# A new order of all 4,839 instructions for a layer of attention and gated feed-forward

## The chip, the cores and the metric

The kernel runs on one core of one Trainium2 chip. The metric is the device time of one execution in microseconds (us), median of several runs. The core has a matrix engine (PE, with its weight loads shown as PEld), a vector engine (DVE), a scalar engine (ACT), GpSimd (POOL), and SyncE (SP), which here only issues DMAs. In this program each works off its own list of instructions in order; one that waits for a semaphore stands in front of all that follow it there.

## The reference

For x of 2048 rows and 512 columns (the factors and biases of the norms are none):

```python
h  = x + A(layernorm(x))                    # attention, 32 heads of 16, 4 segments of 512 rows
h2 = h + (gelu(n @ w_gate) * (n @ w_up)) @ w_down      # n = layernorm(h), inner width 1376
# A, for each segment s and head:
logits = qs @ ks.T * 16**-0.5 + mask        # causal inside the segment
o = g * (phi(qs) @ M) / (phi(qs) @ z + 1e-6) + (1 - g) * softmax(logits) @ vs
M, z = M + phi(ks).T @ vs, z + sum(phi(ks)) # memory of the segments before
# phi(t) = t+1 if t > 0 else exp(t);  g = sigmoid(beta);  at the end o @ wo
```

## The kernel before

All products that need it are made of operands split into a high and a low part ("slot" tiles hold both), three matmuls for one product. The attention is worked off in 16 units U (four columns of heads by four segments), each of two halves Q = 2U, 2U+1:

- `qkv(U)` projects q and k (matmuls of L938), evicts them, and moves them by DMA into the tiles stq and stk (L1062, L1068, L1075); `vproj` makes v (L987, for the first unit L1000).
- `pass_a(Q)` makes the logits once only for the row maxima: matmuls (L1192) into two PSUM banks, and for each block of a bank one DVE reduction (L1202). POOL splits the maxima (L1216, L1217), PE turns them (L1223), and a small DMA writes them into stq (L1230).
- `pass_b(Q)` makes the logits again, transposed (L1250), ACT takes the exponential (L1256), POOL sets the masked triangle to zero (L1264), and PE multiplies by v (L1278, "accum"). Later come the division and the sum with the memory's part (L1311 on DVE, L1317 on POOL).
- `mem(U)` reads the memory (L1140 to L1165).
- `split_weight` and `split_wv` load a weight and split it; for the later weights POOL makes both the high part (L668, L689) and the low part (L675, L694).

Then `wo_seg` makes the output projection, `ln2` the second norm with sums of blocks (L795, L1392, L1398, L1403), and `ffn`/`down` the feed-forward part with a Strassen-like scheme: `prod` (L1537) makes products of three matmuls, ACT copies them (L1544), DVE adds them (L1549), `geglu` (L1555 to L1569) the activation, and `down` (L1602) the last product, which DVE adds to the rows held (L1610). It runs in two halves of 1024 rows, p = 0 and 1.

What is computed, on which engine and from what is fixed by calls of a planner's `op`, which numbers them 0 to 4838 in the order in which the program text makes them (1247 of PE, 1189 of DVE, 1026 of ACT, 751 of POOL, 626 of SP's DMAs; a PE operation is a group of 2 to 32 matmuls). A list of numbers written out in the file, ORDER, then says in which order they are issued. All tiles but constants come from pools, among them the eight PSUM banks; an operation takes its buffers at its place in the order, from those that its predecessors have given back:

```python
        for i in order:
            o = self.ops[i]
            ...
            for v in o.vals:
                if v.t is None and v.pool is not None:
                    p = v.pool
                    v.t = p.free.pop(0)[2]
            ...
            o.fn()                                   # issues the instructions
```

`pass_a` takes two banks for a group of matmuls, and they come back when its DVE reductions are done:

```python
            sas = Val(PA), Val(PA)
            ...
            pe(sum(rr((i + 1) * P) for _, i, _ in cols), prio, f, [sq, sk], sas, acq=[nm], head=0.12, mode="r")
            for a, sa in enumerate(sas):
                for p, i, c0 in cols: ...            # one dve reduction (L1202) per block of the bank
```

The operations that the text names by number:

| number | engine | what |
|---|---|---|
| 5, 6 | SP | loads of the first two blocks of 128 rows of x |
| 2, 3 | POOL, DVE | two iotas (L612, L616); the mask made of them (L622 to L624) |
| 39, 41, 43 | DVE | low parts of the first norm's second half (L907) |
| 93 | POOL | low part of the first wk (L675), read by 102, the first projection (L959) |
| 113 | PE | part of the first projection, reads 39 |
| 123, 122, 124 / 140 | SP | moves of the first q / of the first k |
| 170 | PE | first group of `pass_a(0)` |
| 1461, 1463 | POOL | masks of `pass_b(13)` (L1264), read by 1479, an accum (L1278) |
| 2123, 2124 | POOL | high and low part of a later wv (L689, L694) |
| 2549 | DVE | reciprocal of the denominators of Q = 25 (L1311) |
| 2729, 2735, 2745 | PE | three groups of `pass_a(29)` (L1192) |
| 2736, 2737, 2738, 2739 | DVE | reductions of group 2735 (L1202), two on each of its banks |
| 2609, 2711 | PE | accums of Q = 26 and 27 (L1278) |
| 3066 to 3069 | DVE | normalized rows of `ln2`, one segment (L795) |
| 3838, 3839 | PE, DVE | a `down` product of the first half (L1602) and its addition (L1610) |
| 3842, 3845 | DVE | two more such additions |
| 4051, 4064 / 4055 / 4123 | DVE | block sums of `ln2` (L1392) / a low part (L1403) / a low part of the activation (L1569) |
| 4187 | PE | a `prod` of the second half's first tile (L1537), takes a new bank |
| 4100, 4101, 4105 | PE, ACT, PE | a `prod`, the copy of its bank (L1544), the `prod` that writes the bank again |

Of the kernel before, what the change touches and what calls it, by code (L numbers as in the profile page):

```python
# [56 lines left out]
    0, 6, 5, 100, 1, 10, 9, 8, 12, 7, 28, 13, 14, 91, 16, 4, 76, 11, 92, 27, 18, 29, 30, 15, 17, 31, 88, 89, 32,  # L57
    33, 93, 94, 34, 19, 44, 35, 164, 21, 95, 821, 23, 90, 97, 25, 20, 22, 47, 36, 24, 37, 102, 822, 38, 825, 84,
    77, 46, 103, 104, 82, 26, 110, 42, 826, 96, 43, 105, 39, 81, 111, 167, 40, 827, 106, 112, 823, 98, 107, 113,
    41, 99, 828, 108, 114, 51, 109, 78, 115, 116, 829, 87, 50, 117, 830, 128, 129, 45, 118, 119, 120, 831, 133,  # L60
    48, 121, 144, 631, 145, 123, 134, 122, 146, 49, 147, 832, 80, 135, 833, 139, 138, 52, 124, 834, 165, 53,
    166, 140, 168, 2, 169, 54, 130, 824, 3, 55, 75, 136, 835, 131, 137, 151, 132, 170, 181, 172, 150, 185, 57,
    127, 253, 186, 254, 255, 148, 256, 125, 59, 171, 190, 182, 189, 126, 176, 149, 1024, 184, 85, 58, 188, 1025,
    1027, 56, 152, 836, 187, 153, 257, 101, 74, 161, 163, 154, 837, 183, 180, 60, 1028, 177, 179, 61, 258, 178,
    173, 79, 83, 175, 634, 143, 67, 142, 838, 68, 174, 191, 192, 1029, 141, 62, 818, 259, 69, 260, 2986, 65,
    193, 66, 63, 64, 72, 73, 70, 195, 71, 261, 213, 215, 214, 194, 196, 217, 438, 839, 632, 633, 262, 263, 197,
    198, 199, 270, 216, 439, 440, 625, 272, 229, 840, 441, 239, 273, 1030, 264, 442, 269, 230, 266, 231, 232,
    242, 274, 271, 267, 265, 243, 233, 276, 203, 204, 205, 206, 207, 275, 240, 443, 86, 241, 224, 277, 841, 162,
    444, 227, 225, 268, 226, 234, 628, 842, 237, 278, 445, 200, 201, 245, 202, 238, 228, 843, 235, 248, 236,
    446, 280, 208, 209, 246, 210, 448, 211, 247, 449, 212, 155, 249, 1026, 279, 450, 156, 1031, 218, 447, 244,  # L70
    219, 250, 1032, 844, 220, 292, 221, 845, 222, 846, 157, 1033, 406, 251, 847, 848, 281, 1034, 849, 295, 286,
    294, 293, 288, 852, 287, 282, 635, 636, 1035, 407, 223, 297, 301, 283, 408, 300, 296, 298, 318, 319, 409,
    289, 299, 321, 328, 410, 329, 302, 331, 291, 411, 290, 304, 313, 303, 361, 362, 365, 412, 363, 626, 305,
    627, 314, 306, 307, 308, 316, 323, 413, 364, 320, 324, 353, 355, 354, 326, 414, 815, 1411, 315, 366, 367,
    368, 325, 369, 158, 252, 370, 1036, 797, 1037, 309, 330, 427, 798, 311, 317, 334, 799, 415, 327, 332, 416,
    159, 310, 312, 160, 356, 359, 357, 360, 322, 337, 429, 417, 335, 800, 358, 336, 430, 418, 629, 338, 630,
    421, 333, 1417, 420, 422, 428, 433, 432, 801, 434, 284, 339, 340, 419, 387, 388, 390, 437, 435, 341, 285,
    431, 350, 351, 352, 802, 371, 372, 392, 393, 389, 391, 377, 378, 380, 803, 398, 804, 373, 401, 374, 805,
    482, 375, 483, 484, 485, 486, 586, 376, 395, 396, 806, 426, 379, 394, 809, 587, 808, 477, 1038, 479, 381,
    478, 480, 481, 399, 436, 382, 807, 385, 386, 588, 514, 383, 466, 603, 467, 468, 589, 590, 342, 425, 384,  # L80
    402, 503, 515, 517, 850, 1039, 506, 469, 504, 470, 471, 344, 397, 345, 493, 472, 423, 474, 476, 475, 424,
    473, 507, 505, 400, 343, 494, 516, 496, 495, 591, 498, 592, 508, 346, 347, 497, 487, 501, 488, 541, 502,
    499, 593, 518, 2119, 509, 489, 543, 511, 491, 544, 594, 542, 510, 500, 512, 536, 540, 537, 1040, 348, 490,
    816, 1608, 817, 608, 595, 1041, 539, 545, 403, 492, 609, 597, 598, 538, 596, 610, 513, 614, 457, 615, 458,
    600, 613, 519, 520, 1224, 601, 404, 602, 405, 459, 611, 2113, 533, 599, 1225, 534, 535, 616, 578, 579, 1226,
    605, 781, 567, 581, 570, 571, 530, 1227, 617, 546, 612, 568, 531, 1228, 532, 607, 1042, 606, 549, 550, 572,
    548, 575, 576, 1229, 569, 573, 574, 562, 521, 547, 551, 563, 552, 564, 565, 566, 649, 651, 650, 1230, 557,
    767, 558, 559, 662, 663, 664, 560, 665, 561, 666, 853, 768, 580, 553, 555, 554, 556, 1231, 851, 646, 647,
    648, 1043, 1232, 604, 1233, 652, 653, 654, 655, 656, 785, 1234, 1235, 1236, 769, 657, 659, 660, 1044, 1045,
    658, 770, 673, 674, 771, 676, 661, 577, 582, 618, 460, 583, 688, 683, 584, 522, 523, 1046, 772, 689, 585,  # L90
    1047, 678, 349, 773, 1048, 1049, 1050, 1051, 691, 1052, 727, 819, 675, 820, 729, 667, 692, 677, 728, 731,
    686, 684, 668, 1414, 681, 774, 730, 685, 687, 669, 775, 679, 717, 670, 680, 694, 718, 1420, 719, 671, 690,
    720, 682, 721, 672, 776, 777, 778, 779, 780, 697, 695, 696, 788, 461, 462, 524, 786, 787, 791, 698, 789,
    693, 637, 792, 793, 525, 794, 526, 699, 463, 700, 638, 790, 464, 451, 465, 722, 1605, 1054, 784, 726, 701,
    725, 796, 724, 989, 452, 723, 714, 1609, 453, 1610, 1003, 1055, 795, 715, 738, 1056, 990, 716, 711, 739,
    783, 741, 991, 753, 713, 756, 992, 743, 712, 993, 754, 742, 746, 619, 621, 620, 782, 871, 872, 873, 994,
    759, 995, 879, 880, 881, 882, 883, 755, 747, 732, 740, 744, 527, 702, 748, 996, 762, 733, 760, 874, 875,
    876, 877, 878, 751, 1418, 749, 1419, 734, 997, 736, 854, 761, 745, 735, 884, 885, 886, 887, 888, 1008, 757,
    703, 752, 855, 750, 1010, 737, 1009, 998, 1011, 1014, 758, 2122, 639, 622, 704, 763, 1421, 623, 1422, 705,
    764, 765, 999, 1012, 1191, 856, 868, 869, 870, 857, 859, 860, 2989, 1192, 895, 896, 1013, 858, 528, 898,  # L100
    897, 529, 1193, 900, 901, 1194, 902, 910, 949, 903, 1195, 913, 914, 889, 1001, 890, 766, 953, 911, 905, 906,
    951, 950, 908, 1196, 944, 1197, 952, 706, 891, 916, 945, 1198, 893, 1018, 948, 947, 1015, 946, 917, 936,
    937, 1002, 907, 938, 1199, 861, 909, 919, 892, 899, 862, 904, 624, 1004, 912, 939, 1213, 918, 1214, 943,
    1000, 810, 863, 707, 942, 1200, 1201, 894, 811, 812, 866, 940, 920, 1215, 2995, 915, 941, 867, 864, 1415,
# [1600 lines left out]
```

## Time and profile before

| what | value |
|---|---|
| median of 3 runs | 746.55 us (746.38 to 747.04) |
| the profiled execution's own time | 746.22 us |
| its span, first to last instruction | 744.5 us |
| PE busy | 728.4 us, 98% |
| DVE, ACT, POOL busy | 568.1, 502.7, 485.5 us |

The busy times are sums over all instructions of an engine; the span is what the time follows. An engine's idle time is printed in brackets behind the instruction that ended it, with the instruction on another engine that released it. The busy time of PE counts a matmul to its modelled end, so gaps shorter than a matmul's tail do not show as idle.

### The profile page before, as it was taken

How to read it: one execution, taken by the hardware profiler on the slowest of the kernel's cores; microseconds unless marked ns; L12 is line 12 of the kernel's file. 1: busy time of each engine (PE TensorE's matmuls, PEld its weight loads, DVE VectorE, ACT ScalarE, POOL GpSimd, SP SyncE). 2: the span in 40 equal slices, each digit the busy share in tenths (PEclk: the TensorE clock that was granted, in tenths of full speed). 3: DMA queues.
4: the chain of work that ended last, by engine and by line, in shares of the span. 5: the costliest groups of instructions: out<-in, count | busy, mean ns of one | idle time of the engine just before them, and what ended most of it. 6: DMA issues, size and time to landing. Idle time of an engine off the chain costs nothing.

```text
span 744.5 us, 18739 instructions
## 1 busy us (share of the span) xinstructions
PE 728.4 (98%) x6496; PEld 583.4 (78%) x6496; DVE 568.1 (76%) x1812; ACT 502.7 (68%) x1058; POOL 485.5 (65%) x770
## 2 busy tenths in 40 slices
PE   7999999999999999999999999999999999999997
PEld 6888877877878777876768788888887878888886
DVE  7997889998886898899986656865777666565385
ACT  6888888797767868878685567665685454554540
POOL 6554446565627556897784788759798279659730
PEclk9999999999999999999999999999999999999999
DMA  7755667747666766766768656245353430000003
GB/s 254 216 144 134 175 183 184 192 124 200 165 172 173 210 189 174 216 199 175 206 198 271 231 186 167 56 104 135 120 149 115 145 120 2 0 1 1 0 1 114
DMA packets 89659, 107.93 MB, mean 145 GB/s; under 512 B 31468, under 2 KB 41884, under 8 KB 89564
## 3 DMA queue, kind: packets, MB, share of 16 engines
q1 hardware_dynamic: 89260, 106.34, 50.1%
q8 instruction: 51, 0.84, 0.5%
q10 hardware_dynamic: 304, 0.39, 0.2%
q14 instruction: 44, 0.36, 0.2%
HBM read 57.03 MB, written 23.53 MB: 108 GB/s over the span
## 4 chain that ended last, share of the span: by engine, by line
PE 49%; DVE 2%; ACT 1%; DMA 1%; issue 0%; DVEq 0%; SPq 0%; ACTq 0%
PE bank L1537 27%; PE bank L1602 15%; PE bank L1351 3%; PE bank L1358 2%; PE bank L1278 2%; PE bank L1250 1%; DVE row L1610 1%; DMA stq<-slot 1%; PE bank L1192 0%; DVE row L1564 0%; DVE bank L1392 0%; DVE bank L1562 0%; DVE bank L1549 0%; DVE row L1392 0%; DVE row L1557 0%
## 5 line engine op out<-in xcount | busy, mean ns | idle before, releaser
L1256 ACT ACTIVATE row<-bank 128x512 f32<-128x512 f32 x306 | 163.3, 607 | 34.8 <-PE bank L1250 25.7
L1264 POOL TENSOR_SCALAR_AFFINE_SELECT row<-row 128x256 f32<-128x256 f32 (+1 forms) x306 | 103.9, 363 | 87.7 <-ACT row L1256 82.6
L1202 DVE CUSTOM_DVE_ANT_0 aside<-bank,amask 128x128 f32<-128x128 f32 (+2 forms) x384 | 140.7, 419 | 17.7 <-PE bank L1192 11.7
L938 PE MATMUL bank<-slot,slot 64*128 64x512 f32 x720 | 115.3, 403 | 0.5 <-DVE z L1151 0.2
L1537 PE MATMUL bank<-slot,slot 128*128 128x512 f32 (+1 forms) x357 | 95.2, 390 | 0.7 <-DVE row L1610 0.7
L1202 DVE CUSTOM_DVE_ANT_0 bank<-bank,amask 128x512 f32<-128x512 f32 x128 | 86.3, 711 | 9.9 <-PE bank L1192 8.9
L1192 PE MATMUL bank<-stk,stq 64*128 64x512 f32 (+3 forms) x512 | 83.2, 330 | 2.2 <-DVE bn L726 0.9
L1250 PE MATMUL bank<-stq,stk 64*128 64x384 f32 (+3 forms) x512 | 82.9, 333 | 0.3 <-DVE nm L1202 0.2
L1610 DVE TENSOR_TENSOR row<-row,bank 128x512 f32<-128x512 f32 (+1 forms) x85 | 56.2, 676 | 34.7 <-PE bank L1602 34.1
L938 PEld LDWEIGHTS bank<-slot,slot 64*128 64x128 f32 x720 | 74.9, 185 | 6.8 <-DVE nm L1202 1.3
L1278 PE MATMUL bank<-row,vaug 128*32 128x128 f32 (+3 forms) x978 | 77.9, 436 | 1.3 <-DVE z L1151 0.5
L1537 PEld LDWEIGHTS bank<-slot,slot 128*128 128x128 f32 (+1 forms) x357 | 66.2, 186 | 15.7 <-ACT row L1544 1.1
L1507 POOL TENSOR_TENSOR slot<-row,slot 128x512 fp32r<-128x512 f32 (+2 forms) x43 | 48.1, 1121 | 30.5 <-ACT slot L1505 23.2
L1192 PEld LDWEIGHTS bank<-stk,stq 64*128 64x128 f32 x512 | 57.5, 185 | 13.3 <-DVE nm L1202 5.0
L1250 PEld LDWEIGHTS bank<-stq,stk 64*128 64x128 f32 x512 | 57.4, 185 | 11.9 <-DVE nm L1202 2.8
L1278 PEld LDWEIGHTS bank<-row,vaug 128*32 128x32 f32 x978 | 29.7, 109 | 35.5 <-issue 29.1
L1544 ACT ACTIVATE row<-bank 128x512 f32<-128x512 f32 (+1 forms) x57 | 33.4, 595 | 33.6 <-PE bank L1537 32.8
L987 PE MATMUL bank<-slot,slot 64*128 64x256 f32 x672 | 53.5, 285 | 0.0
L1602 PE MATMUL bank<-slot,slot 128*128 128x512 f32 (+1 forms) x192 | 51.3, 390 | 0.0
L1202 DVE DVE_READ_ACCUMULATOR2_ANT nm<- 128x1 f32 x512 | 50.0, 98 | 0.0
L987 PEld LDWEIGHTS bank<-slot,slot 64*128 64x128 f32 x672 | 48.0, 186 | 1.0 <-DVE nm L1202 0.6
L675 POOL TENSOR_TENSOR slot<-row,slot 128x512 fp32r<-128x512 f32 (+1 forms) x30 | 39.1, 1303 | 5.9 <-ACT ln L880 4.2
(287 smaller groups left out, 1695.4 us busy)
## 6 DMA issues: line engine op xcount, KB each, us to landing
stq<-slot SPq DMA_DIRECT2D x96, 128.0 KB
stk<-slot SPq DMA_DIRECT2D x94, 128.0 KB
row<-x SPq DMA_DIRECT2D x31, 256.0 KB
pv_dram<-row SPq DMA_DIRECT2D x31, 256.0 KB
row<-r_dram SPq DMA_DIRECT2D x26, 256.0 KB
row<-h_dram SPq DMA_DIRECT2D x21, 256.0 KB
row<-wd SPq DMA_DIRECT2D x18, 256.0 KB
row<-wu SPq DMA_DIRECT2D x17, 256.0 KB
```

The costliest lines, as they stand in the source:

```text
L938: return nc.tensor.matmul(pm[i].t, w[i].t[rows_of(r), wi, dc * P:(dc + 1) * P], XT[s][dc].t[rows_of(r), xi, :], start=(dc, wi, xi, ph) == ...
L987: return nc.tensor.matmul(pms[n].t[:, 256 * t:256 * t + 256], XT[s][dc].t[rows_of(r), xi, t0:t0 + P], whl[wi].t[rows_of(r), dc // 2, 256 * ...
L1192: nc.tensor.matmul(sa.t[:, c0:c0 + w], sq.t[own, p, i * P:(i + 1) * P], sk.t[own, p, 0:w], start=True, stop=True, tile_position=(64 * a, 0 ...
L1202: nc.vector.tensor_tensor_reduce(out=(sa.t[:, c0:c0 + w] if i > 2 else aside[:, turns[0]:turns[0] + w]), in0=sa.t[:, c0:c0 + w], in1=amask ...
L1250: nc.tensor.matmul(sc.t[:, c0:c0 + D - q0], sk.t[own, p, q0:q0 + P], sq.t[own, p, q0:D], start=True, stop=True, tile_position=(64 * a, 0), ...
L1256: act(w, prio, lambda sc=sc, e=e: nc.scalar.activation(e.t[:, :w], sc.t[:, :w], AF.Exp), [sc, vtab], [e])
L1264: nc.gpsimd.affine_select(v, v, pattern=pat + [[1, P]], compare_op=OP.is_ge, fill=0.0, base=0, channel_multiplier=-1)
L1278: nc.tensor.matmul(pv.t[32 * n:32 * n + 32, kb * P:D], va.t[:, 136 * kb + 17 * j:136 * kb + 17 * j + 32], e.t[:, lo:lo + D - kb * P], star ...
L1507: pool(0.14 + 2.13e-3 * (hi - lo), prio, lambda: nc.gpsimd.tensor_tensor(v.t[:, 1, :hi - lo], r.t[:, lo:hi], v.t[:, 0, :hi - lo].bitcast(F ...
L1537: nc.tensor.matmul(dst.t[:w], v.t[:, wi, c0 + j * w:c0 + (j + 1) * w], b[bk][j].t[:, xi, :], start=first and j == 0 and n == 0, stop=j == ...
L1602: nc.tensor.matmul(pm.t[:, cs], HH[p, f, s].t[:w, hi, t * P:(t + 1) * P], v.t[:w, wi, cs], start=f == fl[0] and n == 0, stop=f == fl[-1] a ...
L1610: dve(W_, prio, lambda a=a, pm=pm, cs=cs, to=to: nc.vector.tensor_tensor(to.t[:, cs], a.t[:, cs], pm.t[:, cs], op=OP.add), [pm, a], [to])
```

## The change

ORDER is replaced by another permutation of the same numbers. Nothing else differs: not the operations, their engines, shapes or operands, nor the pools. 233 of the 4,839 stand at the same place in the whole list. Seen by engine, 578 of PE's 1247 operations have another rank on their own engine, 875 of DVE's 1189, 750 of ACT's 1026, 646 of POOL's 751 and 549 of SP's 626. Of the 749 PE operations that start before 400 us 173 have another rank, by 0.3 places in the mean over all of them; POOL's there by 3.8 places, SP's by 4.5.

The diff is 260 lines of numbers on each side. Its core, the first lines and a line of each from about 340 us:

```diff
 ORDER = [
-    0, 6, 5, 100, 1, 10, 9, 8, 12, 7, 28, 13, 14, 91, 16, 4, 76, 11, 92, 27, 18, 29, 30, 15, 17, 31, 88, 89, 32,
...
+    4, 5, 9, 76, 6, 10, 100, 12, 0, 11, 8, 1, 28, 77, 13, 7, 14, 27, 29, 16, 15, 18, 91, 17, 92, 88, 821, 45, 2,
...
-    2606, 3067, 3066, 2739, 2738, 2712, 2791, 2685, 2686, 2687, 2703, 2548, 2698, 2658, 3192, 3069, 2549, 2713,
...
+    2656, 2657, 2592, 3061, 2603, 2691, 2692, 3089, 2694, 3189, 2735, 2548, 2685, 2549, 3062, 2550, 2710, 2698,
```

The same at the places that matter below, each engine's own list read out of the two orders:

```
DVE, about 340 us  before 3067 3066 2739 2738 3069 2549 3068 2737 2736 2730 2731
                   after  2549 3062 .. 3065 3066 2738 3068 2739 2736 2737 3067 3069 2746
PE, about 342 us   before 2792 2729 2793 2745 2609 2711     after  2792 2745 2793 2729 2609 2711
DVE, about 565 us  before 4051 3845 4064 4123 3839 4055 4068 3842
                   after  4051 3842 3845 3839 4055 4064
PE, about 565 us   before 4233 3844 4238 4181 3841 3838 4239 4182 4235 4187
                   after  3838 3840 4233 4181 3841 4238 4182 4239 4235 4187
SP, start          before 6 5 8 7 91 88 94 164 821 97 .. 45 48 631 123 122 124 140 824
                   after  5 6 8 7 91 88 821 45 94 97 .. 164 48 824 123 122 140 124 125
DVE, start         before 37 26 826 43 39 827 41 ..  (3 seventeen places later)
                   after  26 37 3 41 39 826 43 827
POOL, start        before 0 100 4 76 93                      after  4 76 100 0 77 2 93
POOL, 180-191 us   before .. 1454 1484 1463 1482 1461 2311   (2123, 2124 follow at 198-200 us)
                   after  2123 1453 2124 1454 1473 .. 1484 1463 1461 2311
PE, about 541 us   before 4100 4096 3884 4097 4105           after  4096 4100 4097 3887 4105
```

516 rows, old and new, of the table ORDER are left out of this document.

## The prediction

> **What bounds the kernel now.** I read the page first, then the busy time by stage, then what PE waited for, then the timeline at each of those waits. By stage:
>
> ```profile
> 0.00:25.00 25.00, 18.80 (x136) 16.72 (x138) 17.75 (x52) 16.91 (x44) 17.16 (x39) 1.00 0.74 239
> 25.00:400.00 375.00, 370.79 (x4870) 289.22 (x4867) 330.24 (x1385) 294.82 (x652) 231.63 (x502) 1.00 0.66 184
> 400.00:550.00 150.00, 150.00 (x662) 122.95 (x661) 97.18 (x183) 98.14 (x193) 114.37 (x111) 1.00 0.53 149
> 550.00:575.00 25.00, 24.31 (x108) 19.83 (x107) 21.68 (x35) 16.14 (x30) 22.66 (x23) 1.00 0.47 137
> 575.00:725.00 150.00, 150.00 (x662) 122.62 (x661) 90.20 (x141) 75.46 (x139) 97.31 (x96) 1.00 0.11 33
> 725.00:744.50 19.50, 14.49 (x70) 12.03 (x68) 11.04 (x19) 1.26 (x2) 2.33 (x2) 0.95 0.30 108
> ```
>
> The columns are length, busy time of PE, PEld, DVE, ACT and POOL with their counts, the granted clock, the share of the DMA engines and GB/s. PE is the bound in every stage and its clock is full. An order cannot shorten a matmul; it can take away PE's idle time, or add to it. That is 6.20 us up to 25 us, 4.21 in the attention (25 to 400), nothing from 400 to 550 and from 575 to 725, 0.69 between these, and 5.01 after 725, together 16.1. Gaps shorter than a matmul's tail are not in these figures.
>
> A second way in which an order costs PE is the change between its three ways of using the array (whole, two row halves, four column strips). Counting the neighbours in PE's two lists gives 81 such changes before and 81 after, in the same kinds, so this term is nothing.
>
> ```profile
> PE bank L875 <- DMA row<-x: 4.4, 1, 4.4
> ```
>
> This is the longest of PE's waits (total, times, longest): the first load of x before anything can run, and it stays. The next three stand at their places below.
>
> **The change, part by part.** Of the thousands of new ranks only those count that move a wait of PE. I went through PE's waits, and asked of each what stands newly ahead of its releaser and what no longer does.
>
> *About 344 us (gain).* Times, durations, then the operation:
>
> ```profile
> 341.45 1.28 POOL L1317 TENSOR_TENSOR row<-row,row 128x512 f32<-128x512 f32 x1
> 341.68 1.34 DVE L795 TENSOR_SCALAR row<-row,mv,ln 128x512 f32<-128x512 f32 x1
> 342.94 0.34 DVE L1311 RECIPROCAL cd<-cd 128x32 f32<-128x32 f32 x1
> ...
> 343.74 0.28 DVE L1202 CUSTOM_DVE_ANT_0 aside<-bank,amask 128x128 f32<-128x128 f32 x1
> 343.94 0.55 DVE L1202 CUSTOM_DVE_ANT_0 aside<-bank,amask 128x384 f32<-128x384 f32 x1
> 344.55 0.50 PE L1192 MATMUL bank<-stk,stq 64*128 64x256 f32 x3 [0.74 <-DVE nm L1202]
> ```
>
> Group 2745 waits for the bank that 2736 gives back at 344.49. Ahead of 2736 stand 3067, 3069 (1.34), 2549 (0.34), 3068 and 2737 (0.28). In the new order 3067, 3069 and 2737 come behind it, 2549 far ahead of this place, and nothing comes in: from 3069 and 2737 alone 1.6 us earlier. The wait of 0.74 is gone. That 2549 comes earlier costs no wait, since the load of its data was issued at 333.1, ten microseconds before:
>
> ```profile
> L1306 SPq DMA_DIRECT2D cd<-pv_dram x1: 542/542/542, 333.1 to 333.1; - x1
> ```
>
> Late next are the reductions of 2745, now behind 3067 and 3069; their cover is the two accums:
>
> ```profile
> 344.98 0.64 PE L1278 MATMUL bank<-vaug,vaug 128*32 128x256 f32 x8
> 345.44 1.90 PE L1278 MATMUL bank<-row,vaug 128*32 128x512 f32 x24
> ...
> L795 DVE TENSOR_SCALAR row<-row,mv,ln x7: 532/621/1341, 339.9 to 381.6; 128x512 f32<-128x512 f32 x7
> ```
>
> Two rows at 0.53 (the shortest) to 0.62 (the median) are 1.1 to 1.2 us against 2.3 of accums (344.98 to 347.3). I take -0.74; the ends are -0.74 and 0.
>
> The row at 341.68 takes 1.34 beside POOL's L1317, which ends at 342.73, where the shortest takes 0.53. [...]
>
> *About 567 us (gain).*
>
> ```profile
> 565.61 0.69 DVE L1392 TENSOR_TENSOR bank<-bank,row 128x512 f32<-128x512 f32 x1
> 566.21 1.00 DVE L1569 TENSOR_TENSOR stk<-row,stk 128x512 fp32r<-128x512 f32 x1
> 567.14 0.67 DVE L1610 TENSOR_TENSOR row<-row,bank 128x512 f32<-128x512 f32 x1
> 567.96 0.94 PE L1537 MATMUL bank<-slot,slot 128*128 128x512 f32 x3 [0.69 <-DVE row L1610]
> ```
>
> 4187 waits for the bank of 3839. In the new order 4064 (0.69) and 4123 (1.00) are behind 3839, and 3842 (0.67) is ahead: 1.0 us earlier. Its matmul 3838 is five groups earlier on PE. The wait of 0.69 is covered; late next would be 4064's banks, which PE's `prod` groups do not read for several groups. I take -0.69; the ends are -0.69 and 0.
>
> *The start.*
>
> ```profile
> 3.04 0.95 POOL L645 MEMSET stq<- 128x1024 f32 x1
> 8.21 1.27 POOL L675 TENSOR_TENSOR slot<-row,slot 128x512 fp32r<-128x512 f32 x1 [4.22 <-ACT ln L880]
> 20.64 0.35 POOL L612 IOTA row<- 128x136 f32 x1
> 20.95 1.52 POOL L616 IOTA row<- 32x136 f32 x4
> 21.03 0.30 DVE L622 CAST bank<-row 128x136 int32<-128x136 f32 x1 [0.79 <-POOL row L612]
> ...
> 22.50 0.30 DVE L624 SCALAR_TENSOR_TENSOR mmask<-bank,row 128x136 f32<-128x136 int32 x1 [0.83 <-POOL row L616]
> 24.03 0.73 PE L1192 MATMUL bank<-stk,stq 64*128 64x512 f32 x6 [0.94 <-DVE bn L726]
> ```
>
> POOL takes a memset (0.95) and the iotas (0.35 + 1.52) ahead of 93: 2.8 us in an idle stretch of 4.22, nothing; uncovered it would cost all of it. DVE takes the mask (three instructions of 0.30) and 41 ahead of 39, and lets 43 and one small statistic go behind. Since 41 and 43 are alike, that is at most 0.9 on the way to 113. Between nothing and 0.9 I take +0.2, nearer the lower end because DVE waits for ACT in this stretch (the row at 11.72 below). At 24.03 PE waits for 170's operands:
>
> ```profile
> 11.72 1.30 DVE L907 TENSOR_TENSOR slot<-bank,slot 128x256 fp32r<-128x256 f32 x3 [0.31 <-ACT slot L905]
> ...
> GB/s 0 82 0 0 0 0 0 0 0 0 0 0 133 215 236 185 195 195 215 225 195 184 246 184 184 215 205 195 185 236 184 164 205 184 215 389 369 359 277 277
> ```
>
> The last row is the DMA rate from 17 to 25 us in 40 slices of 0.2. The six moves of 128 KB flow at some 200 GB/s until 24.0 (slice 35), just when PE starts; the DVE instruction named is only the last event. The new order swaps 124 and 140 inside these six, so the end of the last stays. I take 0, with ends -0.94 (it was DVE after all: the mask's idle 0.79 + 0.83 is gone from 21 to 22.5) and +0.3. The first two loads of x swap too: the first statistics need both, as before.
>
> *POOL's masks (loss).* The largest of five like places:
>
> ```profile
> 190.54 0.90 POOL L1264 TENSOR_SCALAR_AFFINE_SELECT row<-row 128x128 f32<-128x128 f32 x3 [1.12 <-ACT row L1256]
> ...
> 191.99 1.95 PE L1278 MATMUL bank<-row,vaug 128*32 128x512 f32 x24
> 198.45 0.61 POOL L689 CAST slot<-row 128x512 fp32r<-128x512 f32 x1
> 199.15 1.29 POOL L694 TENSOR_TENSOR slot<-row,slot 128x512 fp32r<-128x512 f32 x1
> ```
>
> 2123 and 2124 (0.61 + 1.29) move ahead of 1463 and 1461, whose accum starts 0.55 after the last mask (190.54 + 0.90 = 191.44). Less 0.40 for a mask (1482) that goes behind, 1.50 against 0.55 leaves 0.95, if POOL had no idle time; it had 1.12 just ahead of the last mask. The same sum at four other accums leaves 0.47, 0.20, 0.19 and 0.15 before idle time. Ends 0 and 1.96; I take +0.3, near the lower.
>
> *The rest.* In the feed-forward stages PE never waits, and the covers stay above what they must hide; the shortest falls from three PE groups to two (4100 to 4105), 1.36 us, against one copy by ACT (L1544, below) with two handovers.
>
> ```profile
> 541.41 0.58 ACT L1544 ACTIVATE row<-bank 128x512 f32<-128x512 f32 x1
> ```
>
> Ends 0 and +0.6, if another instruction of that length stands ahead of the copy; I take 0. The last five PE groups and the last four additions are the same, so the tail behind 725 us stays.
>
> The sum: -0.74 - 0.69 + 0 + 0.2 + 0.3 + 0 = -0.93. Against the profiled execution's own 746.22 that is 745.3; the median shown, 746.55, is 0.33 above it, so I predict 745.6.
>
> **The rivals.**
> - *Much faster: the same relief at many small waits.* The attention's 4.21 us of idle, 0.74 of it counted above, is spread over dozens of waits, mostly for banks, and DVE's and ACT's lists are changed all along it. If half of the other 3.5 goes, 1.7 more: 743.9. Against it: at most of the waits that I followed, the releaser has the same operations ahead.
> - *No change: given back.* PE's next operands come by DMA, as at 24 us, and being early means waiting there: 746.5. For it: DMA share 0.66 in the attention. Against it: one wait only of the list names a landing.
> - *Slower: POOL's queue decides.* If POOL, in order, has no idle time where weights were pulled forward, all 1.96 is paid and the gains are not seen: 748.5. It decides from the point where the idle time ahead of the masks is below the 1.9 of a pair of copies. Against it: POOL is busy 231.63 of 375.
>
> **How the numbers follow.** The forecast, 745.6 with its own range of 744.8 to 746.4, gets 0.47; much faster 0.19, given back 0.23, slower 0.11. The range over 8 in 10 reaches to 743.8 and 747.4; it leaves out the slower case and the far end of the first. A measurement can tell about 0.2%, 1.5 us: faster means below 745.06. That is a third of the forecast's case (0.16) and all of much faster: 0.35. Slower (above 748.04) is 0.11, the rest 0.54.
>
> **What would show it.** The L1192 matmul near 344 us and the L1537 near 567 us without their 0.74 and 0.69; the first L1192 still near 24.0 to 24.3; the accums of Q = 13 near 192 us with a wait for POOL of at most 0.3; 81 changes of PE's use. The prediction is wrong if PE's idle from 25 to 400 us falls below 2.5 or rises above 5, or if a new wait appears in the feed-forward stages.

## The result and the profile after

| | median | range | executions |
|---|---|---|---|
| before | 746.5 us | 746.38 to 747.04 | 4 |
| after | 751.66 us | 751.54 to 751.98 | 4 |
| after / before | 1.0068 | 95%: 1.0051 to 1.0086 | |

The new order was slower by 5.2 us here, where 745.6 was forecast and 747.4 was the upper end. The profiled execution took 751.98 us with a span of 750.3. A later measurement of the same kernel (below) showed that this is one of two groups of times that it has; what follows explains the long one first.

The busy time by stage of the kernel after, columns as in the prediction:

```profile
0.00:25.00 25.00, 19.12 (x128) 17.26 (x129) 16.34 (x51) 16.61 (x41) 18.17 (x42) 1.00 0.74 233
25.00:400.00 375.00, 369.64 (x4863) 287.13 (x4864) 329.41 (x1382) 294.31 (x652) 228.52 (x498) 1.00 0.66 182
550.00:575.00 25.00, 25.00 (x112) 20.50 (x110) 22.51 (x33) 17.85 (x34) 24.30 (x24) 1.00 0.39 116
575.00:725.00 150.00, 146.84 (x639) 119.55 (x638) 89.96 (x138) 73.16 (x134) 94.78 (x94) 0.99 0.11 37
```

PE's idle time up to 400 us went from 6.20 + 4.21 to 5.88 + 5.36, the 0.69 between 550 and 575 is gone, and a stage that had none, 575 to 725, now has 3.16. The longest waits of PE say the same:

```profile
PE bank L875 <- DMA row<-x: 3.8, 1, 3.8
PE bank L1537 <- DVE slot L1403: 3.2, 1, 3.2
PE bank L1223 <- DVE nm L1202: 1.0, 1, 1.0
PE bank L1192 <- DMA stq<-slot: 1.0, 1, 1.0
```

The second is new, and the third stands where the prediction took a wait away. The timeline of PE, DVE and POOL around the second one:

```profile
574.93 0.39 PE L1537 MATMUL bank<-slot,slot 128*128 128x512 f32 x1
578.47 1.80 PE L1537 MATMUL bank<-slot,slot 128*128 128x512 f32 x5 [3.16 <-DVE slot L1403]
...
572.33 4.89 DVE L1569 TENSOR_TENSOR slot<-row,slot 128x512 fp32r<-128x512 f32 x1
577.14 0.68 DVE L1392 TENSOR_TENSOR bank<-stq,bank 128x512 f32<-128x512 f32 x1
577.74 0.68 DVE L1403 TENSOR_TENSOR slot<-bank,slot 128x512 fp32r<-128x512 f32 x1
...
571.25 1.28 POOL L1403 TENSOR_TENSOR slot<-row,slot 128x512 fp32r<-128x512 f32 x1
572.50 1.28 POOL L675 TENSOR_TENSOR stk<-row,stk 128x512 fp32r<-128x512 f32 x1
573.75 1.28 POOL L1569 TENSOR_TENSOR slot<-row,slot 128x512 fp32r<-128x512 f32 x1
575.00 0.72 POOL L1514 TENSOR_TENSOR vaug<-row,vaug 128x256 f32<-128x256 f32 x1
575.68 0.99 POOL L1507 TENSOR_TENSOR slot<-row,slot 128x384 fp32r<-128x384 f32 x1
```

One DVE subtraction, 4123, the low part of the activation for the inner tile f = 9 and the second 512 rows of the first half, lasts 4.89 us instead of the 1.00 it took at 566.21 in the profile before. Both its inputs are in SBUF. Beside it run five POOL instructions without a gap, the last of which ends at 576.67; 4123 ends at 577.22, 0.55 us later. What stands behind it on DVE, a block sum (L1392) and a low part (L1403), is then late, and PE waits 3.16 us for the latter. The wait has a second bill, to be read in the granted clock (the sixth figure behind the length, counts in brackets left out; PE's busy time is the first):

```profile
575.00:578.40 3.40, 0.32 (x2) 0.00 (x0) 3.40 (x4) 0.00 (x0) 1.67 (x3) 1.00 0.37 139
578.40:580.00 1.60, 1.53 (x5) 1.26 (x6) 1.56 (x4) 0.60 (x1) 0.00 (x0) 0.80 0.00 0
580.00:581.30 1.30, 1.30 (x4) 0.99 (x3) 1.12 (x3) 0.60 (x1) 0.00 (x0) 0.50 0.00 0
581.30:582.60 1.30, 1.30 (x4) 0.99 (x3) 1.30 (x3) 0.00 (x0) 0.00 (x0) 0.50 0.00 0
582.60:585.00 2.40, 2.40 (x12) 1.96 (x11) 0.42 (x1) 0.60 (x1) 0.00 (x0) 0.96 0.29 109
```

Behind the idle stretch the clock is 0.50 for 2.6 us, and the slices before and behind, 0.80 and 0.96 in the mean, are in part at 0.50 too: from 579.36 to 582.77, 3.41 us together. Groups of three matmuls then take 1.28 us from start to start instead of 0.68. Until the old pace is back this costs 1.75 us; with the wait, 3.3 us from start to start beyond the usual step, that makes the 5.06 of the table below. In the 3.41 us up to 579.36 PE was idle for 2.52, and in another long profile below (the one with six copies on DVE) for 2.13 of the 3.41 us ahead of its slow stretch. How long a pause it takes, and what sets the length of the slow stretch, the traces do not show.

Counting both, the same places of PE's list tell where the 5.8 us between the two spans arose (start of each PE group less that of the group of the same rank before):

| stretch (before's time) | shift in it | what is there |
|---|---|---|
| to 24 us | +0.86 | start |
| 24 to 74 | +0.58 | |
| 74 to 176 | -1.62 | |
| 176 to 337 | +1.41 | |
| 337 to 383 | +1.71 | ln2's rows among the last reductions |
| 383 to 560 | +0.06 | |
| 560 to 572 | -0.89 | the wait of 4187 is gone |
| 572 to 589 | +5.06 | the stall of 4123 |
| 589 to the last PE group | +0.06 | |
| behind it | -1.4 | last additions and stores: 5.5 us from the start of the last PE group before, 4.1 after |

So the stall is most of the difference. Of the rest, the shifts before 400 us vary from one profile to the next by some 2 us: at 383 us PE is 0.7 to 2.9 us late in the twelve profiles that have the new order up to there.

### The profile page after: what moved, and what is told of

It reads as the page before. It is cut to its first block, busy times and chain, and to the rows that moved or that the text cites. A ratio compares the mean times of both kernels' runs of the same rounds, so it can differ in the third digit from the quotient of the medians.

```text
span 750.3 us, 18713 instructions
## 1 busy us (share of the span) xinstructions
PE 732.3 (98%) x6496; PEld 585.2 (78%) x6496; DVE 570.0 (76%) x1812; ACT 504.3 (67%) x1058; POOL 484.7 (65%) x770
## 4 chain that ended last, share of the span: by engine, by line
PE 83%; DVE 6%; POOL 4%; issue 2%; DMA 2%; ACT 2%; SPq 0%; DVEq 0%; POOLq 0%; ACTq 0%
PE bank L1537 28%; PE bank L1602 16%; PE bank L938 8%; PE bank L1278 7%; PE bank L987 5%; PE bank L1250 5%; PE bank L1192 5%; PE bank L1351 3%; PE bank L1358 2%; DVE aside L1202 2%; DVE bank L1202 1%; POOL row L1264 1%; PE bank L1160 1%; DMA row<-r_dram 1%; POOL slot L675 1%
## 5 line engine op out<-in xcount | busy, mean ns | idle before, releaser
L938 PE MATMUL bank<-slot,slot 64*128 64x512 f32 x720 | 113.0, 401 | 0.2 <-DVE z L1151 0.2
L1537 PE MATMUL bank<-slot,slot 128*128 128x512 f32 (+1 forms) x333 | 91.5, 394 | 3.2 <-DVE slot L1403 3.2
L1507 POOL TENSOR_TENSOR slot<-row,slot 128x512 fp32r<-128x512 f32 (+3 forms) x58 | 65.4, 1134 | 27.3 <-ACT slot L1505 26.0
L1192 PE MATMUL bank<-stk,stq 64*128 64x512 f32 (+3 forms) x512 | 80.9, 330 | 2.0 <-DMA stq<-slot 1.0
L1250 PE MATMUL bank<-stq,stk 64*128 64x512 f32 (+3 forms) x512 | 82.0, 335 | 0.6 <-DMA stq<-mx 0.2
L1278 PE MATMUL bank<-row,vaug 128*32 128x512 f32 (+3 forms) x982 | 77.9, 437 | 1.1 <-DVE z L1151 0.4
L1537 PEld LDWEIGHTS bank<-slot,slot 128*128 128x128 f32 (+1 forms) x333 | 62.1, 187 | 17.9 <-DVE slot L1403 3.6
L1610 DVE TENSOR_TENSOR row<-row,bank 128x512 f32<-128x512 f32 (+1 forms) x79 | 52.0, 675 | 30.9 <-PE bank L1602 30.7
L1192 PEld LDWEIGHTS bank<-stk,stq 64*128 64x128 f32 x512 | 56.6, 185 | 13.3 <-DVE nm L1202 4.2
L1602 PE MATMUL bank<-slot,slot 128*128 128x512 f32 (+2 forms) x231 | 60.6, 387 | 0.0
L1602 PEld LDWEIGHTS bank<-slot,slot 128*128 128x128 f32 (+1 forms) x231 | 42.9, 188 | 9.3 <-DVE row L1564 0.2
L1537 PE MATMUL bank<-stk,slot 128*128 128x512 f32 (+1 forms) x177 | 49.2, 391 | 0.0
```

Source lines behind the costliest of these rows:

```text
L938: return nc.tensor.matmul(pm[i].t, w[i].t[rows_of(r), wi, dc * P:(dc + 1) * P], XT[s][dc].t[rows_of(r), xi, :], start=(dc, wi, xi, ph) == ...
L1192: nc.tensor.matmul(sa.t[:, c0:c0 + w], sq.t[own, p, i * P:(i + 1) * P], sk.t[own, p, 0:w], start=True, stop=True, tile_position=(64 * a, 0 ...
L1250: nc.tensor.matmul(sc.t[:, c0:c0 + D - q0], sk.t[own, p, q0:q0 + P], sq.t[own, p, q0:D], start=True, stop=True, tile_position=(64 * a, 0), ...
L1278: nc.tensor.matmul(pv.t[32 * n:32 * n + 32, kb * P:D], va.t[:, 136 * kb + 17 * j:136 * kb + 17 * j + 32], e.t[:, lo:lo + D - kb * P], star ...
L1507: pool(0.14 + 2.13e-3 * (hi - lo), prio, lambda: nc.gpsimd.tensor_tensor(v.t[:, 1, :hi - lo], r.t[:, lo:hi], v.t[:, 0, :hi - lo].bitcast(F ...
L1537: nc.tensor.matmul(dst.t[:w], v.t[:, wi, c0 + j * w:c0 + (j + 1) * w], b[bk][j].t[:, xi, :], start=first and j == 0 and n == 0, stop=j == ...
```

## The experiments

The kernels have extra lines, so their L numbers run up to five above those of after (L1572 to L1575 are L1569, L1407 is L1403). A "gap" is a pause of POOL. Orders are shown by name or as one engine's list; the files have the numbers written out. The ratios are to before, measured beside each kernel; they follow the means of the executions, not the medians given. Before itself lay between 745.8 and 749.21 us there, with medians from 746.53 to 747.26.

**Which part of the order costs the time.** Two orders were cut together at 480 us, where both have worked off the same operations for PE.

```diff
-ORDER = new
+ORDER = segments(before to 480 us, new after)      # e1_late_new
+ORDER = segments(new to 480 us, before after)      # e2_early_new
```

> The order of before up to 480 us, the new order from there on. If nearly all of the loss is the one stall at 575 to 583 us (5.0 us there, less the 0.85 us gained at 568), this kernel takes 746.5 + 4.1 = 750.6 us and shows a DVE subtraction (L1569) of more than 4 us near 572. If instead the new order loses in the attention and the later place only shows what was lost before (a rest of buffers or DMAs that come later), the time is below 748 us and that subtraction takes 0.7 us.

> The new order up to 480 us, the order of before from there on. PE stood 2.95 us later at that point in the new kernel, so 746.5 + 3.0 = 749.5 us if the two parts add up. If the attention's lateness is absorbed later (a wait that is there anyway, as the 0.7 us at 567), 748.7 or less.

The late part alone gave 746.36 us (ratio 0.9995, 0.9977 to 1.0014): nine executions between 745.4 and 746.83, and one of 752.34. The early part alone gave 746.93 (1.0, 0.9986 to 1.0013), none above 749.22. As medians, neither the 750.6 nor the 749.5 us came. In the profile of the first, one of its short executions, 4123 was let in by the end of one POOL instruction:

```profile
570.51 0.73 DVE L1569 TENSOR_TENSOR stk<-row,stk 128x512 fp32r<-128x512 f32 x1
572.44 1.75 DVE L1569 TENSOR_TENSOR slot<-row,slot 128x512 fp32r<-128x512 f32 x1
```

So the early part costs nothing to be seen, and the late part does not have its 5 us in every execution.

**A pause of POOL.** 4123 and the order stay; POOL, ahead of its subtraction 3799 (L675), copies one element per row of what 4123 writes, and so has to wait for it.

```diff
+            if room:                       # only for the weight of (p, f) = (0, 9); room = (0, 9, 1)
+                nc.gpsimd.tensor_copy(tick, HH[room].t[:, 1, 0:1].bitcast(F32))
             nc.gpsimd.tensor_tensor(v.t[:rows, 1, :w], r.t[:rows, :w], ...)     # 3799
```

> The new order, with one more POOL instruction: a copy of 128x1 ahead of the L675 that starts at 572.50, which reads what DVE's long L1569 writes, so that POOL waits for DVE there. Port theory (DVE's subtraction with both inputs in SBUF can't start while POOL's instructions follow each other without a break, 566 to 576.7 us): the subtraction takes about 0.9 us instead of 4.89, the stall of 3.45 us and most of the 1.5 us behind it go, and the kernel gains 4 to 5 us although POOL gets an instruction and a wait more: 747.0 to 747.7 us. Queue theory (group 4194 waits because too much stands ahead of its operand in DVE's and ACT's lists): no change, 751.7 us, or worse by the 0.7 us that POOL waits.

746.76 us, 745.08 to 747.55 in ten executions; 0.9994 (0.9983 to 1.0005). The timeline of DVE and POOL:

```profile
572.39 0.73 DVE L1574 TENSOR_TENSOR slot<-row,slot 128x512 fp32r<-128x512 f32 x1
...
573.19 0.19 POOL L677 COPY tick<-slot 128x1 f32<-128x1 f32 x1 [0.61 <-DVE slot L1574]
573.33 1.30 POOL L678 TENSOR_TENSOR stk<-row,stk 128x512 fp32r<-128x512 f32 x1
```

4123 asks at the same place and takes 0.73. With this pause no execution was long, in this kernel and in three more below, 38 together: POOL's chain is what held it.

**The subtraction earlier on DVE.** 4123 stands right behind 4051, seven places up, nearer to where it stood before.

```diff
-DVE  4051 3842 3845 3839 4055 4064 .. 4123
+DVE  4051 4123 3842 3845 3839 4055 4064 ..
```

> The new order, with DVE's long L1569 (4123) moved up by seven places to where it stood before relative to 4051. Queue theory: the operands of 4194 come as early as before and the kernel is near 747.5 us. Port theory: POOL's chain is unbroken at 568.4 too, until 4066 has to wait for 4065 and so for DVE itself, at 571.3; the subtraction takes about 3 us there, everything behind it on DVE is late by that, and PE waits about 3.5 us at group 4187 instead of at 4194: 750 us or more.

746.59 us (745.72 to 748.35; 0.9998, 0.9988 to 1.0008). 4123 took 1.04 us at 567.62, until the end of one POOL instruction. That agrees with a stall that belongs to the place. But the figures that either theory gave were missed: 747.5 us by the one, 3 us for the subtraction and 750 us or more by the other. The late part alone had one long execution in ten, so ten without one do not show that this kernel has none.

**The changed kernel once more.** No edit: 4 executions of one group do not show how often another occurs.

> The changed kernel once more, with more runs. Theory A (the long L1569 depends on nanoseconds between DVE's request and the ends of POOL's instructions, so that it comes in some executions only): two groups of times, one near 746.5 us and one near 752 us, nothing between. Theory B (it belongs to this order): all runs near 751.7 us.

746.41 us as the median of 12, ratio 1.0013 (0.9993 to 1.0033): eight between 745.39 and 746.94, and four of 749.9, 750.92, 751.52 and 751.76. With the four of the first measurement, 8 of 16 executions are long. The profile fell on a long one, 750.92:

```profile
571.29 4.89 DVE L1569 TENSOR_TENSOR slot<-row,slot 128x512 fp32r<-128x512 f32 x1
...
577.44 1.62 PE L1537 MATMUL bank<-slot,slot 128*128 128x512 f32 x5 [3.16 <-DVE slot L1403]
```

The same stall, to the hundredth. Where it does not occur, the kernel is not slower than before (746.85).

**DVE beside POOL by itself.** Not the layer: ACT releases a row of seven POOL subtractions and a DVE instruction, the latter moved along the row, first in steps of 17 ns (e6), then in steps of 2 to 4 about an instruction's end (e9). The core of it:

```python
        nc.gpsimd.tensor_tensor(po[0], go, xb, op=OP.subtract)
        for i in range(1, n):
            nc.gpsimd.tensor_tensor(po[i], xa, xb, op=OP.subtract)
        nc.vector.tensor_tensor(do[1][:, 0:w], go[:, 0:w], bank[:, 0:w], op=OP.add)   # its width sets the time
        nc.vector.tensor_tensor(do[0], dx, dy, op=OP.subtract)                        # the one measured
```

> Not the layer, a measurement by itself: 76 times, POOL does seven subtractions of 128x512 without a break, and DVE asks for one 128x512 instruction at an instant that moves by 17 ns from case to case. If DVE always gets in at the end of the POOL instruction that runs, its two-input subtraction takes 0.6 to 1.95 us in every case. If it can lose several ends in a row, some cases take 3 us and more, up to 8. An instruction with one input in PSUM takes 0.68 us in all cases, the one in the form of L795 behaves as the two-input one.

> Not the layer. The measurement with seven POOL subtractions again, with DVE's request in steps of 2 to 4 ns from 260 ns ahead of the end of a POOL instruction to 60 ns behind it, once plain and once with waits for ACT on POOL's and DVE's instructions as the layer has them. Theory A (a request that falls on the hand-over from one POOL instruction to the next is lost, and then loses the following ends too): in a part of this range the subtraction takes 3 us and more, up to 8. If it only misses the one end: 2.0 us there and never more; then what made 4.9 us in the layer is not this and stays open.

The groups of the first of them (count, then busy time and mean ns of one):

```profile
L50 DVE TENSOR_TENSOR do<-dx,dy 128x512 f32<-128x512 f32 x65 | 79.4, 1222 | 0.0
L54 DVE TENSOR_SCALAR do<-dx,dy 128x512 f32<-128x512 f32 x12 | 8.8, 734 | 0.0
L52 DVE TENSOR_TENSOR do<-dx,bank 128x512 f32<-128x512 f32 x3 | 2.0, 680 | 0.0
```

With one input in PSUM an instruction took 0.68 in the mean of three cases, as L1392 did at 577.14 above with POOL idle. With both in SBUF each one that found POOL busy was let in at the end of the instruction then running, 0.73 to 1.78 us in all. The second measurement found when that end is missed: 15 of 190 cases, all of which asked within 35 ns of it, took 1.77 to 1.80, one end more; the form of L795 missed it where it asked less than some 150 ns ahead (18 of 39 cases, at most 1.65). More than one end was never lost. An instant that falls into such a window, which was what I expected, does not make 4.89 us.

**Longer chain.** The last POOL instruction of the chain, a low part 128 x 384 (L1507), is done four times.

```diff
+            def low():
+                for _ in range(times):      # 4 for the first part of (p, f) = (1, 10)
                     nc.gpsimd.tensor_tensor(v.t[:, 1, :hi - lo], r.t[:, lo:hi], ...)
```

> The new order; POOL does the last subtraction of its chain (L1507, 128x384, 0.99 us) four times instead of once, some 2.9 us more at the chain's end. Theory A (in the slow executions DVE's subtraction waits until POOL's chain ends): the slow group of times moves from 750-752 up to 753-755 us, the fast group stays near 746.4. Theory B (in the slow executions DVE waits for something else that happens to end with the chain): the slow group stays at 750-752. If the slow group vanishes, the repeats leave a gap in the chain (each waits for the one before).

750.22 us (1.0043, 1.0023 to 1.0063), in three groups: two executions at 744.74 and 745.52, seven from 749.22 to 751.18, three from 752.12 to 753.59. The profile fell on one of the two: there 4123, at 570.95, was let in at the first end and took 0.73, so the same place can go well with nothing changed ahead of it. Long executions are more (10 of 12), but only three are longer still. This decides nothing: in the profile POOL stands idle for 0.08 us ahead of each repeat, which waits for the one before, so the longer chain was not an unbroken one.

**A later request.** One, three or six copies of 128 x 1 on DVE right ahead of 4123.

```diff
         def add(c, src, dst, late=0):
...
+                for _ in range(late):               # 1, 3, 6; only for g0 of (p, f) = (1, 1)
+                    nc.vector.tensor_copy(tock, dst.t[:, 0:1])
```

> The new order with one DVE copy of 128x1 ahead of the long L1569, so that its request comes about 0.1 to 0.2 us later, close to or behind the hand-over at 572.5 us. If the instant of the request decides: the share of slow executions changes from 4 in 12 to none or to nearly all. If it does not: a third stay slow.

> The same with three such copies, 0.3 to 0.5 us later: the request falls into the middle of the next POOL instruction, where it won in every case of the measurements by themselves. If the instant decides: no slow execution, DVE's subtraction takes 1.0 to 1.8 us, 746.5 us. If not: a third stay slow.

> The same with six copies, 0.6 to 1.0 us later: as with three.

751.28 (1.0058, 1.0039 to 1.0078), 751.09 (1.006, 1.004 to 1.008) and 751.2 us (1.006, 1.0047 to 1.0073); of the 13 executions twelve lie between 748.92 and 753.72, and one at 748.19, little above before's highest there, 748.08. None is in the short group of the changed kernel. The subtraction in the three profiles, and POOL's chain in the second:

```profile
570.64 4.65 DVE L1572 TENSOR_TENSOR slot<-row,slot 128x512 fp32r<-128x512 f32 x1
```

```profile
571.42 4.28 DVE L1572 TENSOR_TENSOR slot<-row,slot 128x512 fp32r<-128x512 f32 x1
...
570.96 1.32 POOL L675 TENSOR_TENSOR stk<-row,stk 128x512 fp32r<-128x512 f32 x1
572.21 1.31 POOL L1572 TENSOR_TENSOR slot<-row,slot 128x512 fp32r<-128x512 f32 x1
573.45 0.75 POOL L1514 TENSOR_TENSOR vaug<-row,vaug 128x256 f32<-128x256 f32 x1
574.14 1.01 POOL L1507 TENSOR_TENSOR slot<-row,slot 128x384 fp32r<-128x384 f32 x1
```

```profile
571.78 3.69 DVE L1572 TENSOR_TENSOR slot<-row,slot 128x512 fp32r<-128x512 f32 x1
```

With three copies the request comes at 571.42, 0.85 us ahead of the end of the running instruction and so nowhere near an edge, and three ends go by. The later it asks, the shorter it takes, for it ends at the same event: in all five long profiles 0.549 to 0.554 us behind the end of the chain's last instruction. That only a request near an end can lose has fallen; that 4123 waits for the chain's end stands. Why with the copies hardly an execution is short, instead of half of them, is not known: a third was expected if the instant plays no part, and the copies change more than the instant.

**Semaphore waits.** In the measurements by themselves so far each of POOL's subtractions carried a wait for a semaphore. In the layer's chain two of those behind 4123's request do (L675, L1514) and two do not (L1569, L1507). The same measurement with waits at some, all or none of the six places behind the first subtraction:

```python
    for pattern in ("nnnnnn", "wwwwww", "nwwwww", "wnnnnn", "nnwnnn", "nnnnww"):      # w: with a wait
```

> Not the layer. 48 chains of seven POOL subtractions; in a chain each of the last six either carries a wait for an ACT copy that has long been done (w) or carries none (n): nnnnnn (its last one waits for POOL itself), wwwwww, nwwwww, wnnnnn, nnwnnn, nnnnww, each with DVE's request at four instants of the first POOL instruction and in two forms. Theory A (POOL keeps the port over an instruction without a wait; DVE gets in at the first end whose successor carries one): wwwwww and wnnnnn 0.9 to 1.8 us, nwwwww 2.2 to 3.1, nnwnnn 3.4 to 4.3, nnnnww about 6, nnnnnn 7 to 8. Theory B (once lost, DVE waits for the end of the chain): as A where the first successor waits, and 7 to 8 us in the other four. Theory C (waits play no part): all 0.9 to 1.8 us, as in the measurements before, all of whose POOL instructions carried waits.

All 48 cases were let in at the first end, in 1.07 to 1.79 us. In the layer, with the three copies on DVE as above, a POOL copy of 128 x 1 was set between 3799 and the next subtraction, once reading something that it had to ask a semaphore for (long given), once something that it need not:

```diff
+            if (p, f, s) == (0, 8, 1):
+                nc.gpsimd.tensor_copy(tick, HH[0, 9, 0].t[:, 0, 0:1].bitcast(F32))   # e17_mark_wait
+                nc.gpsimd.tensor_copy(tick, e.t[:, 0:1])                             # e18_mark_free
```

> The kernel with three more DVE copies, slow in all its four executions, with a POOL copy of 128x1 between 3799 and 3908, at whose end DVE lost; it carries a wait for an ACT instruction done 2 us before. Theories A and B: DVE gets in ahead of this copy, its subtraction takes at most 1.8 us, all executions near 746.7 us. Theory C: 749 to 753 us as without it.

> The same with a copy that carries no wait, since it reads what the next subtraction reads. Theories A and B: 749 to 753 us, DVE's subtraction above 3.5 us. Theory C: as with the copy that waits.

748.02 us both (1.0011, 1.0 to 1.0023; 1.0002, 0.9991 to 1.0014), 20 executions up to 749.55, where the three copies alone had 748.92 to 753.72. In the profile with the wait and in that without:

```profile
572.36 1.38 DVE L1575 TENSOR_TENSOR slot<-row,slot 128x512 fp32r<-128x512 f32 x1
...
573.14 0.65 POOL L1574 COPY tick<-slot 128x1 f32<-128x1 f32 x1
```

```profile
572.65 1.42 DVE L1575 TENSOR_TENSOR slot<-row,slot 128x512 fp32r<-128x512 f32 x1
575.19 2.38 DVE L1575 TENSOR_TENSOR slot<-row,slot 128x512 fp32r<-128x512 f32 x1
```

In these profiles either copy lets 4123 in, so a wait plays no part: A and B are out. But C, too, was wrong in that the copy that waits would change nothing. The times stay 1.3 us above the 746.7 expected, and of the first kernel the profile is the fastest execution. In the second profile the next subtraction of the same kind (4116, at 575.19) still loses two ends, up to the end of the chain.

**The wait at 344 us.** Once in the new order with the gap, 2739 ahead of 3068; once in the order before, with only the reductions 2737 and 2736 ahead of 3069 and 3068, and 2549 ahead of 3067.

```diff
-DVE  3066 2738 3068 2739 2736 2737 3067 3069           # new order (e8_swap)
+DVE  3066 2738 2739 3068 2736 2737 3067 3069
-DVE  3067 3066 2739 2738 3069 2549 3068 2737 2736      # order before (e10_b344)
+DVE  2549 3067 3066 2739 2738 2737 2736 3069 3068
```

> The new order with POOL's wait of before, and in DVE's list 2739 ahead of 3068 as in the old order. If the 1.0 us that PE waits at 344 us comes from 3068 (L795, 1.66 us beside POOL) standing ahead of 2739: that wait falls below 0.2 us and the kernel is 1 us faster than the same without the swap, 745.8 against 746.8. If the bank is late for another reason: no change.

> The old order with one place changed as the forecast read it: in DVE's list 2738, 2737, 2736 stand ahead of 3069 and 3068, and 2549 ahead of 3067. If the wait at 344 us is the term of 0.74 us that the forecast took: 746.6 - 0.7 = 745.9 us and the wait is gone. If PE then waits at the next group whose releaser stands behind 3069: no change.

The first gave 746.18 us (0.9992, 0.9983 to 1.0001): the wait of 1.0 at L1223 went, and one of 0.79 came at 2745, which takes the bank that 2736, still behind 3068, gives back. So of the 1.0 us expected 0.6 came (746.76 without the move). The second gave 745.23 (0.9975, 0.9966 to 0.9985), 1.7 us below its neighbours of before; at the place itself PE gains 1.2 us between the two profiles. Its timeline:

```profile
342.87 1.11 DVE L795 TENSOR_SCALAR row<-row,mv,ln 128x512 f32<-128x512 f32 x2
...
344.04 0.42 PE L1192 MATMUL bank<-stk,stq 64*128 64x256 f32 x4
```

The group 2745 starts without a wait, and the two rows behind the reductions take 1.11 together, the estimate of 1.1 to 1.2.

**A version out of both.** Before's order to 74 us, the new one to 176, before's to 480, the new one after, with the gap (e7); the same with the move at 344 us (e11).

```diff
+ORDER = segments(before to 74 us, new to 176, before to 480, new after)      # and the gap: e7_best
+DVE  2549 3067 3066 2739 2738 2737 2736 .. 3069 3068                         # e11_best2 besides
```

> Before's order up to 74 us, the new one from there to 176 us (where PE gained 1.4 us in the new kernel), before's to 480 us, the new one after that (0.85 us gained at 568 us), with POOL's wait of the run with one more POOL instruction. If the gains of the stretches add up: 746.6 - 1.4 - 0.9 = 744.3 us. If a gain depends on what came ahead of it: between that and 746.6.

> The fastest kernel so far (stretches of the old and the new order, and POOL's wait) with that place changed too. If it adds up: 744.7 - 0.7 = 744.0 us.

744.66 us (0.9977, 0.9969 to 0.9986) and 743.27 (0.9951, 0.9939 to 0.9964), the best of all. PE's longest stages in the latter:

```profile
25.00:400.00 375.00, 371.51 (x4878) 291.72 (x4879) 329.51 (x1385) 295.26 (x654) 231.53 (x503) 1.00 0.66 185
...
550.00:575.00 25.00, 25.00 (x111) 20.56 (x110) 22.55 (x36) 16.34 (x30) 24.09 (x24) 1.00 0.41 125
575.00:725.00 150.00, 150.00 (x661) 122.56 (x661) 89.98 (x141) 75.48 (x138) 98.17 (x95) 1.00 0.10 34
```

In the attention 3.49 of idle is left, and none from 550 to 725. In 38 executions with the gap (e3, e7, e8, e11) the highest is 747.55: no long one.

## Why the prediction was wrong

**The step that failed** stands under "The rest": "In the feed-forward stages PE never waits, and the covers stay above what they must hide", taken at 0 with ends 0 and +0.6; in half of the executions of the changed kernel nothing is to be seen of a loss, and in the profiles of the others it is +5.06: a wait of 3.16 us and the half clock behind it. That 4123 would leave its place ahead of 3839 was counted; the place to which it went was not looked at. There POOL has an unbroken chain of five instructions, and 4123, with two inputs in SBUF, was held over all of them. At 344 us I had read from the profile before that a row of L795 took 1.34 beside a POOL instruction, where the shortest takes 0.53, and did not ask what POOL does beside the other moved instructions. Held over one POOL instruction, 4123 would have taken at most 1.8 us (1.78 was the most in the first measurement by itself), which the cover would have held (in e1, it took 1.75 and PE did not wait). In the trace the holder was not one instruction but the chain: 4.89.

**About 567 us**, -0.69: right. No wait at L1537 for L1610 is left, and the stretch from 560 to 572 shrank by 0.86 to 0.89 in six profiles that have the new order there.

**About 344 us**, -0.74: the mechanism was right and the term is still wrong. The wait of 0.74 went, and in before's order the move alone is worth 1.7 us by the medians and 1.2 at the place, more than the term. But I wrote "nothing comes in", and looked only at 2736. In the new list 3068 stands ahead of 2739, which releases the transposition ahead of 2745. The timeline of the kernel after:

```profile
342.34 1.66 DVE L795 TENSOR_SCALAR row<-row,mv,ln 128x512 f32<-128x512 f32 x1
343.92 0.28 DVE L1202 CUSTOM_DVE_ANT_0 aside<-bank,amask 128x128 f32<-128x128 f32 x1
...
344.26 0.23 PE L1223 MATMUL bank<-ident,mm 64*32 64x64 f32 x1 [1.04 <-DVE nm L1202]
...
342.44 1.28 POOL L1317 TENSOR_TENSOR row<-row,row 128x512 f32<-128x512 f32 x1
```

3068, which asked 0.1 us ahead of POOL's L1317, took 1.66 where the prediction's own row for this case had 1.34, and PE waited 1.04. The two rows behind the reductions, put at 1.1 to 1.2, took 2.14 beside another POOL instruction (L1507); no wait above 0.2 us came of that. The stretch from 337 to 383 lost 1.4 to 1.9 in the profiles with this order (1.1 with 2739 ahead of 3068) instead of gaining 0.74.

**The start**, +0.2: too small, as far as the scatter tells. With the new order the first matmul starts 0.5 to 0.8 earlier, since the first load of x lands earlier, and the way from there to the first L1192 is 0.6 to 2.5 longer than in the profile of before. The net is -0.1 to +1.9 in twelve profiles (mean +1.0), where four others with the old start have -0.2 to +1.1 (mean +0.4). POOL's iotas are hidden, as said; the first L1192 waits for a landing, at 24.88 instead of 24.0 to 24.3. Which part makes the way longer is open.

```profile
24.88 0.50 PE L1192 MATMUL bank<-stk,stq 64*128 64x512 f32 x2 [1.01 <-DMA stq<-slot]
192.27 1.95 PE L1278 MATMUL bank<-row,vaug 128*32 128x512 f32 x24
```

**POOL's masks**, +0.3: 0. The second row is the accum of Q = 13; it follows without a wait. The changes of PE's use, too, came as said, 81 in either profile. That one costs time can be read in the profile of before: after a matmul of 128 x 256 in column strips the next one started 0.31 us behind its start at each of 24 changes to row halves, and at most 0.22 behind it where no change followed. The rival "POOL's queue decides", 748.5, had the right engine and the wrong place: POOL held no matmul through its own queue, but it held 4123 on DVE, for 4.89 us.

**Not forecast**: a gain of 0.9 to 1.6 between 74 and 176 us in each profile with the new order there, of the kind that the rival "much faster" gave without a place; losses of up to 1.4 from 176 to 337; and a tail, which was to stay, that is 1.5 us shorter (3.5 instead of 5.0 from the end of the last matmul, in all eleven profiles with the whole new order; why is open). All this about balances: without the stall the kernel with the gap measured 746.76 beside 746.77, and the eight short executions of the changed kernel have a median of 746.0 beside 746.85. Between 0 and -0.8 against the -0.93 forecast, the other terms together are not what put the time outside the range. That the short executions come so near to the forecast is luck: the term at 344 us had the wrong sign, and gains that I had not forecast made up for it. PE's idle time from 25 to 400 us, 5.36, was above the bound of 5, and the new wait in the feed-forward stages was the other sign named.

**What stays open**: why in the layer several ends in a row are lost, in half of the executions of one and the same program, where some 350 cases by themselves lost one at most. Neither a request near an end nor the waits of POOL's instructions explain it. Other addresses of the operands, and PE and ACT busy beside it, were not tried. The "port" of the expectations is my name for whatever holds DVE beside POOL; the traces show only when the instructions start and end.

## What to carry to other kernels

A moved instruction has a price at its new place, not only a gain at its old one: list for each moved DVE instruction with two inputs in SBUF what POOL does beside it, and where POOL has several instructions without a pause, count the whole chain as what it may cost (4.89 us here), not one of them (up to 1.78). Where it matters, break the chain with a POOL instruction that waits for DVE's result, which cost nothing measurable here (746.76 us beside 746.77). A tiny one without that wait let 4123 in as well (1.38 and 1.42 us), but in one profile the next subtraction was then held (2.38). A kernel whose times fall into two groups needs ten executions or more, and a profile of each group, before a median means anything.

## What the runs showed of the hardware

A DVE subtraction of 128 x 512 with both inputs in SBUF was held over up to five POOL instructions, and ended 0.549 to 0.554 us behind the last of them, in five profiles; where it got in at the first end, it ended 0.544 to 0.554 behind that. By itself it lost one end more in 15 of 190 cases, all of which asked within 35 ns of that end, and the form of L795 in 18 of 39, within some 150 ns. A pause of PE of 3.12 to 3.16 us was followed by half the clock in each of the five long profiles: for 3.41 us, with a further loss of 1.7 to 1.75 us, in four of them; in the one with a single copy on DVE ahead of 4123 the groups of PE ran at half the pace from 576.55 to 582.67, with a loss of 3.0.
